# One hand-written order against another: 1498 operations of an attention and channel-mix kernel on five engines

## The chip, the cores and the metric

The kernel runs on one core of a Trainium2 chip. The metric is the device time of one execution in microseconds (us). A core has five engines that run at the same time, each through its own sequence of instructions: TensorE (PE, with its weight loads as PEld), VectorE (DVE), ScalarE (ACT), GpSimd (POOL) and SyncE (SP, which here only issues transfers). An instruction waits until what it reads is there and the buffer that it writes is free, and everything behind it on its engine waits with it. Transfers run on 16 DMA engines.

## The reference

For 8 batches of 8 heads, 576 positions and 64 features, linear attention with a feature map is followed by a channel mix with a shift by one position:

```python
def phi(x):
    proj = np.einsum('bhsd,df->bhsf', x, w_phi)
    proj = proj - np.max(np.abs(proj), axis=-1, keepdims=True)
    return np.concatenate([np.exp(proj), np.exp(-proj)], axis=-1)
q_p, k_p = (phi(q), phi(k))
kv = np.einsum('bhsf,bhsd->bhfd', k_p, v)
z = np.sum(k_p, axis=2)
num = np.einsum('bhsf,bhfd->bhsd', q_p, kv)
den = np.einsum('bhsf,bhf->bhs', q_p, z)[..., None] + 1e-06
...
xk = mu_k * x + (1.0 - mu_k) * x_prev
xr = mu_r * x + (1.0 - mu_r) * x_prev
k = np.maximum(xk @ w_k, 0.0)
v = k * k @ w_v
r = 1.0 / (1.0 + np.exp(-(xr @ w_r)))
return (r * v).astype(np.float32)
```

Here x is num / den with the heads side by side (512 wide); w_k is 512 x 1024, w_v 1024 x 512, w_r 512 x 512.

## The kernel before

The functions `add_load`, `add_edge`, `add_pair`, `add_moe` and `add_moe_edge` (from L312 on) make named operations. The text `ORDER` (L19) is one list of all 1498 names, written out in full by a search that is not part of the kernel. `Plan.order` (L143) reads it, and the last loop (L980) issues the operations in that sequence, so each engine's own sequence is what remains of the list when the other engines' names are left out. In a word such as `pb1/DVE`, what stands behind the slash is the engine, where there is a choice; `:1` is the PSUM buffer that the operation writes; `+2@3` puts two filler matmuls in front. A name that ends in `.d` stands for the landing of a transfer; except for `lk0.0.d` and `lq0.0.d`, which are casts, it issues nothing.

The work is 32 pairs of heads, four to a batch (pair n is of batch n // 4). For a pair:

- lk, lq, lv load k, q and v. lk and lq are always on POOL and write bfloat16 (L321); the loads of k, q for the very first pair (hk, hq) come on SP and ACT and are cast afterwards. lv is on POOL or SP (L327), in halves of a batch (three buffers), except that the first three loads of batch 0 are pair 0, pair 1 and pairs 2 and 3.
- The transposes of batches 0 and 1 are on TensorE (pt, L338) with copies out of PSUM (pa, pb, L346); those of the other six are DMA transposes by SP (tr, L352), two pairs each.
- kp and qp project k and q (L566); rk and rq reduce to the negative largest magnitude (L579, L584); ea and eb take exp of both signs of k (L605); em does it for the maxima of k (L591); mh, mt and mc bring the maxima of q across (L615, L620); qt projects q transposed and adds the maxima (L630, L636), qa and qb take exp (L643); va and vb scale v (L597); kv, kc, nd form the products (L656, L677); ra, rd divide (L685, L689). The last 64 of the 576 positions of a batch, for all its pairs, are handled by the edge operations tp, rt, mhe, mte, mce, eme, ekt, qte, eqe (L457 to L515).
- The result is transposed to put features on partitions: for pairs 0 to 7 by TensorE (xt, L715, copied by xe, xf), for the others by a DMA transpose on SP (xz, L700, with xu, L704 to L708). df takes the difference to the shifted position (L726), xa and xb mix (L732).

For a batch b, whose four pairs must all be mixed: h{b}.0 to .7 (L810) with rl (relu, L206, L208) and sq (square, L212, L214), r{b}.0 to .3 (L829) with th (tanh, L835), v{b}.0 to .3 (L843) with ob (L849) and the stores so on SP (L856). For each two batches the edge rows do the same once more: he, rle, sqe, re, the, ve, obe, soe (L897 to L942).

TensorE's 64-row operations are kp, qp, qt, kv, tp and qte; the others use all 128 rows. PSUM has three buffers P and two M, so h, r, v, pt, mt, xt and the like alternate between two.

Of the kernel before, what the change touches and what calls it, by code (L numbers as in the profile page):

```python
# [19 lines left out]
ones hk hq ident dve2 hk.d hq.d wphi wphi.d lk0.1 lk0.1.d lq0.1 lq0.1.d mus mus.d lk0.2 lk0.2.d dve3  # L20
lq0.2 lq0.2.d lv0.0/POOL lv0.0.d lk0.0.d/DVE lq0.0.d/ACT lv0.1/SP lv0.1.d pt0.0:0+9@0 lv0.2/SP
lv0.2.d pt0.1:1 pa0/DVE pb0/ACT tr0 dve1 tp0.0:0+1@2 kp0:1 rt0.0 qp0:2 rk0 eme0.0 mhe0.0/POOL ekt0.0
pt1.0:1+1@0 lk1.0 lk1.0.d pa1/ACT mte0.0:0 rq0 ea0 lq1.0 lq1.0.d pt1.1:1+2@2 pb1/DVE tr1 lk1.2
lk1.2.d eb0 kp1:2+2@2 tp0.1:0 lq1.2 lq1.2.d rt0.1 em0 rk1 qp1:1+1@1 ekt0.1 mh0/POOL eme0.1 wk.0
wk.0.d mt0:1+1@1 mc0/ACT mce0.0/DVE rq1 ea1 qt0:0+1@2 wk.1 wk.1.d wk.d pt2.0:1 qa0 pt2.1:0
mhe0.1/DVE mh1/POOL pa2/DVE pb2/DVE tr2 eb1 vb0/POOL pt3.0:1+2@3 pt3.1:0 pa3/DVE qb0 pb3/DVE tr3
va0/POOL mte0.1:1+1@3 qp2:2 mt1:0 rq2 qp3:1 mce0.1/ACT mc1/ACT em1 qte0.1:1 wr.0 wr.0.d qt1:0 eqe0.1
qte0.0:0 rq3 lv1.0/POOL lv1.0.d qa1 tp0.2:2 va1/POOL qb1 rt0.2 kp2:1+3@1 rk2 vb1/POOL ekt0.2
kv0:0+1@1 eqe0.0 pt4.0:1 kc0/DVE ea2 mhe0.2/POOL pt4.1:0 pa4/DVE kp3:0 pb4/DVE tr4 kv1:2 wr.1 wr.1.d
wr.d eb2 rk3 pt5.0:0 wv.0 wv.0.d pt5.1:1 eme0.2 qp4:1 pa5/DVE kc1/ACT mh2/POOL em2 rq4 nd0:2  # L30
mh3/POOL pb5/ACT tr5 wv.1 wv.1.d wv.d em3 mt2:0 pt6.0:1 ea3 mc2/DVE ra0 nd1:1 vb2/POOL pa6/DVE rd0
eb3 pt6.1:0 pt7.0:1 va2/POOL pb6/DVE tr6 qt2:2 pa7/ACT ra1 rd1 mte0.2:0 qa2 lk2.0 lk2.0.d pt7.1:1
mce0.2/DVE qp5:0 pb7/DVE tr7 qte0.2:0 lq2.0 lq2.0.d qb2 rq5 tp1.0:1 xt0:1 va3/POOL eqe0.2 kv2:2
rt1.0 xf0/ACT xe0/ACT kp4:0 mh4/POOL mt3:0 kc2/ACT rk4 xt1:1 df0/POOL mc3/ACT ekt1.0 nd2:2 ra2 ea4
vb3/POOL xe1/DVE qt3:1+1@0 rd2 mt4:0 xf1/ACT mc4/ACT df1/DVE qa3 xt2:1 xa0 kv3:2 eb4 mhe1.0/DVE
xe2/DVE mte1.0:0+1@0 xb0 kc3/ACT kp5:0 qb3 qt4:2 xa1 eme1.0 xf2/DVE nd3:1 rk5 mce1.0/ACT df2/POOL
qa4 ra3 qb4 rd3 lv1.2/POOL lv1.2.d ea5 xa2 xt3:0+7@1 qp6:2 xb1 qte1.0:1 xe3/ACT qp7:1 eb5 xf3/DVE
df3/DVE xa3 em4 qt5:0+1@0 eqe1.0 rq6 vb4/POOL h0.0:0 qa5 va4/POOL rq7 kp6:2 qb5 h0.1:1 rk6 mh6/POOL
kp7:1 rl0.1/ACT kv4:0 va5/POOL rl0.0/ACT tr2.0 tr2.0.d tr8 tr9 mt6:1 kc4/DVE ea6 h0.2:0 rk7 vb5/POOL
eb6 xb2 kv5:0+1@2 mc6/ACT sq0.0/ACT xb3 nd4:2 tr2.2 tr2.2.d tr10 tr11 em6 ea7 h0.3:1 kc5/DVE  # L40
vb6/POOL ra4 rd4 nd5:0 eb7 vb7/POOL rl0.3/DVE qt6:2 rl0.2/ACT ra5 qp8:1 rd5 qa6 lv2.0/SP lv2.0.d
sq0.1/POOL r0.0:1 rq8 qb6 va6/POOL qp9:0 h0.4:0 rq9 th0.0 sq0.3/POOL sq0.2/ACT qt7:2 kv6:1 rl0.4/DVE
qa7 lk3.0 lk3.0.d tp2.0:0 kc6/DVE h0.5:1 mh8/POOL rt2.0 qb7 va7/POOL xt4:0 rl0.5/ACT kp8:1 xf4/DVE
# [973 lines left out]
```

## Time and profile before

| what | value |
|---|---|
| device time, three runs | 277.23, 278.66 (median), 284.07 us |
| span of the profiled execution | 275.3 us |
| instructions | 8865 |
| first transpose on TensorE (pt0.0) | 5.2 us |
| second pair's transpose (pt1.0) | 7.6 us |
| first product of the channel mix (h0.0) | 39.6 us |
| last product ends, last engine instruction ends | 271.0, 271.5 us |
| granted TensorE clock | 1.000 |
| read from HBM, written | 33.62 MB, 9.44 MB |
| DMA transposes of q and k, on SP | 12, issue 2.4 to 5.9 us each |
| POOL load issues | 31, 0.56 to 0.81 us each |

The span is counted from the first to the last instruction of the profiled execution. The page gives no device time of that one execution beside it; the runs' times are from executions without the profiler. A busy share counts the time in which an engine executes; waiting and issuing from SP don't count. Matmuls overlap, so that a busy TensorE needn't be one at its peak.

### The profile page before, as it was taken

The numbers are of one execution on the slowest core, as the hardware profiler recorded it, in microseconds if no ns is written. First come the engines' busy times: TensorE is split into PE (matmuls) and PEld (weight loads), VectorE is DVE, ScalarE is ACT, GpSimd is POOL, SyncE is SP. The second block draws the span as 40 slices with busy tenths as digits, with TensorE's granted clock in tenths as the row PEclk, the third lists the DMA queues.
The fourth block names the chain that finished last, engine by engine and source line by source line (L and its number), as shares of the span: only waits on it lengthen the run. The fifth ranks groups of instructions, "written<-read, shape, count | busy, mean of one in ns | idle before, by whom it ended". The sixth has DMA issues, their size and how long they took to land.

```text
span 275.3 us, 8865 instructions
## 1 busy us (share of the span) xinstructions
PE 261.7 (95%) x3682; PEld 154.1 (56%) x3730; DVE 234.6 (85%) x388; ACT 223.1 (81%) x413; POOL 142.4 (52%) x193
## 2 busy tenths in 40 slices
PE   7899889999899999999999999999999999999993
PEld 3567656566555566555565666555566565444542
DVE  6999999999799989999999889998889897864222
ACT  3899999999899997899898999789987777616330
POOL 5799557976818682633459465821931611300200
PEclk9999999999999999999999999999999999999999
DMA  7999999599999899759699998981725324142134
GB/s 147 285 209 250 209 213 174 114 235 175 238 129 200 202 219 185 155 127 248 99 166 164 215 249 142 171 255 41 161 89 88 77 52 100 42 110 67 29 88 116
DMA packets 65817, 42.89 MB, mean 156 GB/s; under 512 B 47152, under 2 KB 57008, under 8 KB 65776
## 3 DMA queue, kind: packets, MB, share of 16 engines
q1 hardware_dynamic: 54496, 27.54, 49.3%
q0 software_dynamic: 11056, 14.42, 29.1%
q8 instruction: 29, 0.48, 0.8%
q10 hardware_dynamic: 224, 0.36, 0.5%
q14 instruction: 12, 0.10, 0.1%
HBM read 33.62 MB, written 9.44 MB: 156 GB/s over the span
## 4 chain that ended last, share of the span: by engine, by line
PE 75%; DVE 8%; ACT 6%; issue 4%; DMA 3%; POOL 2%; SPq 0%; POOLq 0%; ACTq 0%
PE ps_h L810 19%; PE ps_v L843 17%; PE ps_r L829 9%; PE ps_nd L677 5%; PE ps_kv L656 5%; DMA qkT<-nat 3%; PE ps_he L897 3%; PE ps_ve L929 3%; PE ps_k L566 2%; PE ps_qT L630 2%; PE ps_q L566 2%; PE ps_qT L636 2%; ACT k L605 2%; DVE nmk L579 2%; PE ps_f L292 1%
## 5 line engine op out<-in xcount | busy, mean ns | idle before, releaser
L597 POOL TENSOR_TENSOR v<-vt,v 128x576 bf16<-128x576 f32 x59 | 69.8, 1203 | 33.5 <-ACT v L591 31.1
L605 ACT ACTIVATE k<-ps_k 128x1024 bf16<-128x1024 f32 x64 | 64.8, 1047 | 1.3 <-DVE nmk L579 1.3
L643 ACT ACTIVATE q<-ps_qT 128x1024 bf16<-128x1024 f32 x64 | 63.8, 1054 | 1.8 <-PE ps_qT L636 1.7
L810 PE MATMUL ps_h<-xk,wk_bf 128*128 128x512 bf16 x235 | 60.5, 380 | 1.2
L843 PE MATMUL ps_v<-wv_bf,kk 128*128 128x512 bf16 x244 | 58.2, 379 | 0.6
L579 DVE TENSOR_REDUCE nmk<-ps_k 128x8 f32<-128x1024 f32 x32 | 38.8, 1217 | 1.8 <-PE ps_k L566 1.5
L584 DVE TENSOR_REDUCE nmq<-ps_q 128x8 f32<-128x1024 f32 x32 | 38.3, 1217 | 1.6 <-PE ps_q L566 1.4
L843 PEld LDWEIGHTS <-kk 128*128 128x128 bf16 x256 | 24.1, 98 | 27.3
L810 PEld LDWEIGHTS <-wk_bf 128*128 128x128 bf16 x256 | 22.7, 97 | 25.0 <-issue 0.7
L206 ACT ACTIVATE krelu<-ps_h 128x512 bf16<-128x512 f32 x48 | 28.8, 611 | 9.3 <-PE ps_h L810 9.3
L726 POOL TENSOR_TENSOR diff<-xs 128x576 bf16<-128x576 bf16 x15 | 20.2, 1346 | 28.8 <-ACT xs L706 12.7
L214 POOL TENSOR_TENSOR kk<-krelu 128x512 bf16<-128x512 bf16 x18 | 19.1, 1068 | 30.3 <-ACT krelu L206 26.6
L849 DVE SCALAR_TENSOR_TENSOR ob<-rt,ps_v 128x512 f32<-128x512 bf16 x32 | 21.7, 682 | 14.3 <-PE ps_v L843 12.7
L829 PE MATMUL ps_r<-wr_bf,xr 128*128 128x512 bf16 x116 | 31.1, 380 | 0.7
L835 ACT ACTIVATE rt<-ps_r 128x512 bf16<-128x512 f32 x32 | 19.7, 615 | 8.8 <-PE ps_r L829 8.7
L732 DVE SCALAR_TENSOR_TENSOR xk<-diff,mu_k_t,xs 128x576 bf16<-128x576 bf16 x32 | 26.7, 839 | 0.1
L689 DVE TENSOR_TENSOR x_sc<-ps_nd,rden 128x640 bf16<-128x640 f32 x32 | 26.0, 817 | 0.6
L732 DVE SCALAR_TENSOR_TENSOR xr<-diff,mu_r_t,xs 128x576 bf16<-128x576 bf16 x32 | 25.6, 806 | 0.1
L656 PE MATMUL ps_kv<-v,k 64*128 64x65 bf16 x1024 | 22.4, 190 | 0.5 <-ACT q L643 0.2
L566 PEld LDWEIGHTS <-qkT 64*128 64x128 bf16 x512 | 16.5, 94 | 11.0 <-issue 8.0
L656 PEld LDWEIGHTS <-k 64*128 64x128 bf16 x1024 | 19.3, 94 | 5.7 <-issue 1.8
L677 PE MATMUL ps_nd<-kv,q 128*128 128x65 bf16 x512 | 21.4, 193 | 0.0
(102 smaller groups left out, 414.3 us busy)
## 6 DMA issues: line engine op xcount, KB each, us to landing
out_dram<-ob SPq DMA_DIRECT2D x70, 128.0 KB, 2.5
vt<-in_v_dram SPq DMA_DIRECT2D x11, 576.0 KB, 6.1
nat<-in_k_dram POOLq DMA_DIRECT2D x6, 576.0 KB, 7.8
nat<-in_q_dram POOLq DMA_DIRECT2D x6, 576.0 KB, 8.0
vt<-in_v_dram POOLq DMA_DIRECT2D x4, 576.0 KB, 6.0
wk_bf<-in_moe_w_k_dram POOLq DMA_DIRECT2D x2, 512.0 KB, 11.4
wv_bf<-in_moe_w_v_dram POOLq DMA_DIRECT2D x2, 512.0 KB, 10.6
nat<-in_k_dram POOLq DMA_DIRECT2D x3, 288.0 KB, 6.9
```

The lines of the kernel that those rows point to most:

```text
L206: nc.scalar.activation(out_, in_, AF.Relu, scale=HALF)
L579: nc.vector.tensor_reduce(t[:, j, :], s["k"].rearrange("p a (g f) -> p (a g) f", f=128), axis=AX.X, op=ALU.max, apply_absolute_value=True, ...
L584: nc.vector.tensor_reduce(t[:, j, :], s["q"].rearrange("p a (g f) -> p (a g) f", f=128), axis=AX.X, op=ALU.max, apply_absolute_value=True, ...
L597: (nc.vector if eng == "DVE" else nc.gpsimd).tensor_tensor(vb[:, a, pn, :, 0:64], vt[b, a // 2][:, a % 2, :].rearrange("p (s d) -> p s d", ...
L605: nc.scalar.activation(s[f"k{pn}"], s["k"].rearrange("p a (g f) -> p (a g) f", f=128), AF.Exp, scale=(1.0 if pn == 0 else -1.0))
L643: nc.scalar.activation(t.rearrange("f x (a p) -> f x a p", a=2), s["qT"].rearrange("f a (x p) -> f x a p", p=64), AF.Exp, scale=(1.0 if pn ...
L656: nc.tensor.matmul(ps[:, hh, pn * 65:(pn + 1) * 65], lhsT=s[f"k{pn}"][r, c, :], rhs=vb[r, a, pn, 2 * g + par, :], start=(pn == 0 and c == ...
L677: nc.tensor.matmul(ps[:, bk, o * 65:(o + 1) * 65], lhsT=tail if sl < 2 else s[f"q{pn}"][:, 2 * G + h, :], rhs=s["kv"][:, h, pn, :], start= ...
L732: nc.vector.scalar_tensor_tensor(out=t[:, a, (b % 2) * S:(b % 2 + 1) * S], in0=s["d"], scalar=mu[:, a:a + 1], in1=xs[:, a, 0:S], op0=ALU.m ...
L810: nc.tensor.matmul(ps, lhsT=wk_bf[:, c, fc * 128:(fc + 1) * 128], rhs=xkt[bp][:, c, m0:m0 + 512], start=(c == 0), stop=(c == NDC - 1))
L829: nc.tensor.matmul(ps, lhsT=xrt[bp][:, c, m0 + ci * 128:m0 + (ci + 1) * 128], rhs=wr_bf[:, c, :], start=(c == 0), stop=(c == NDC - 1))
L843: nc.tensor.matmul(ps, lhsT=s["kk"][:, fc, ci * 128:(ci + 1) * 128], rhs=wv_bf[:, fc, :], start=(fc == 0), stop=(fc == NFC - 1))
```

## The change

Only the text `ORDER` differs. The set of names is the same, the 17 places with filler matmuls and their numbers too. What differs is the sequence on every engine and the engine of some operations:

| operation | before | after |
|---|---|---|
| lv | POOL 5, SP 12 | POOL 11, SP 6 |
| rl, rle | ACT 53, DVE 19 | ACT 49, DVE 23 |
| sq, sqe | ACT 28, DVE 26, POOL 18 | ACT 29, DVE 21, POOL 22 |
| va, vb | POOL 59, DVE 5 | POOL 55, DVE 9 |
| df | DVE 17, POOL 15 | DVE 15, POOL 17 |
| xu | ACT 12, POOL 10, DVE 2 | ACT 5, POOL 16, DVE 3 |
| xe, xf | ACT 6, DVE 10 | ACT 3, DVE 13 |
| kc | ACT 19, DVE 13 | ACT 21, DVE 11 |
| mc, mce | ACT 17, DVE 11 | ACT 12, DVE 16 |
| mh, mhe | POOL 22, DVE 6 | POOL 24, DVE 4 |
| pa, pb | ACT 4, DVE 12 | ACT 5, DVE 11 |
| cast of lq0.0 | ACT | DVE |

TensorE's sequence is close to the old one: most moves are by one to three places; tr7.2 now comes before tr7.0 on SP. The diff, cut to the parts that the text speaks of:

```diff
-ones hk hq ident dve2 hk.d hq.d wphi wphi.d lk0.1 lk0.1.d lq0.1 lq0.1.d mus mus.d lk0.2 lk0.2.d dve3
-lq0.2 lq0.2.d lv0.0/POOL lv0.0.d lk0.0.d/DVE lq0.0.d/ACT lv0.1/SP lv0.1.d pt0.0:0+9@0 lv0.2/SP
-lv0.2.d pt0.1:1 pa0/DVE pb0/ACT tr0 dve1 tp0.0:0+1@2 kp0:1 rt0.0 qp0:2 rk0 eme0.0 mhe0.0/POOL ekt0.0
-pt1.0:1+1@0 lk1.0 lk1.0.d pa1/ACT mte0.0:0 rq0 ea0 lq1.0 lq1.0.d pt1.1:1+2@2 pb1/DVE tr1 lk1.2
...
-qa7 lk3.0 lk3.0.d tp2.0:0 kc6/DVE h0.5:1 mh8/POOL rt2.0 qb7 va7/POOL xt4:0 rl0.5/ACT kp8:1 xf4/DVE
-xe4/DVE qp10:2 eme2.0 lq3.0 lq3.0.d r0.1:1 rk8 ekt2.0 mhe2.0/POOL r0.2:0 th0.1 rq10 sq0.4/POOL ea8
...
-rk11 ea10 lk4.0 lk4.0.d v0.1:0 qb8 mh10/DVE xa5 lv3.0/SP lv3.0.d eb10 xb5 kv9:0 xb4 em10 qt9:1
...
-ob5.3 xu29/ACT xu28/ACT rd30 nd31:0 the2 df28/POOL r6.0:0 xz30 xz30.d ra31 df29/DVE h6.1:1 th6.0
...
-xu31/ACT soe2 soe2.d df31/DVE r6.2:1 ob6.0 xb30 so6.0 so6.0.d r6.3:0 th6.2 xa31 v6.1:1 th6.3 xb31
-v6.2:0 ob6.1 so6.1 so6.1.d r7.0:1 ob6.2 xa30 so6.2 so6.2.d r7.1:0 th7.0 h7.0:1 th7.1 h7.1:0
...
+hk wphi mus wphi.d mus.d hq ident lv0.1/POOL lk0.1 lq0.1 lk0.1.d lq0.1.d lv0.1.d ones dve2 dve3 hk.d
+hq.d lk0.0.d/DVE lq0.0.d/DVE pt0.0:0+9@0 pa0/DVE dve1 pt0.1:1 pb0/ACT tr0 tp0.0:0+1@2 rt0.0 ekt0.0
+eme0.0 kp0:1 pt1.0:1+1@0 qp0:2 pa1/ACT rk0 ea0 eb0 rq0 lk0.2 lv0.0/POOL lq0.2 lk0.2.d lq0.2.d
+lv0.0.d em0 mhe0.0/POOL lk1.0 lq1.0 lk1.2 mh0/POOL lv0.2/POOL lk1.0.d pt1.1:1+2@2 pb1/DVE tr1
...
+wk.1 qa1 qb1 kv0:0+1@1 rk2 pa4/ACT ekt0.2 ea2 eme0.2 eb2 pt4.1:1 pt5.0:0 kc0/DVE pb4/DVE pa5/DVE tr4
+kp3:0 kv1:1 pt5.1:0 rk3 pt7.0:1 kc1/ACT qp4:2 pb5/DVE pa7/DVE pt6.0:0 mt2:1 nd0:1 em2 ea3 mc2/ACT
...
+xe4/DVE sq0.5/DVE r0.1:0 th0.1 kc7/DVE rk8 qp10:1 kp9:0 h0.6:1 rq10 rk9 lk3.0 mhe2.0/POOL lq3.0
+lk3.0.d df4/POOL mh8/POOL sq0.4/POOL lq3.0.d xa4 ea8 rl0.6/ACT eb8 r0.2:0 qp11:1 h0.7:1 em8 va8/POOL
...
+tr13 tr3.2.d tr14 tr15 xe5/DVE rk10 xf5/DVE sq0.7/POOL vb9/POOL va9/POOL mh10/POOL df5/POOL lk4.0
...
+qt30:2 th5.3 so4.3.d v5.3:0 rl6.0/ACT qa30 eb31 qb30 re2:1 the2 vb30/DVE kv30:1 kv31:2 qt31:0 ob5.3
+xz28 xz29 so5.2 so5.1 so5.0 xz29.d xz28.d r6.0:0 h6.1:1 xu28/ACT df28/POOL kc31/ACT th6.0 xu29/POOL
+df29/POOL kc30/DVE sqe2.1/DVE sq6.0/DVE rl6.1/DVE qa31 sq6.1/ACT qb31 h6.2:0 nd30:1 rl6.2/DVE xb29
+sq6.2/ACT h6.3:1 xb28 rl6.3/ACT sq6.3/ACT h6.4:0 rl6.4/DVE ra30 sq6.4/POOL nd31:2 h6.5:1 rl6.5/ACT
...
+r6.2:1 xu31/ACT th6.2 r6.3:0 v6.1:1 th6.3 v6.2:0 df31/DVE xb31 df30/DVE xa30 ob6.1 xb30 ob6.2 xa31
+so6.0 soe2 so6.0.d soe2.d r7.0:1 r7.1:0 th7.0 th7.1 h7.0:1 rl7.0/ACT sq7.0/DVE h7.1:0 h7.2:1
```

## The prediction

> **What bounds the kernel now.** I read the page's busy shares and slices first, then the sums by stretch of time, then the waits of TensorE, then the timeline of the first 14 us and of the end.
>
> Page, busy shares and three rows of slices:
>
> ```profile
> PE 261.7 (95%) x3682; PEld 154.1 (56%) x3730; DVE 234.6 (85%) x388; ACT 223.1 (81%) x413; POOL 142.4 (52%) x193
> PE   7899889999899999999999999999999999999993
> DVE  6999999999799989999999889998889897864222
> ACT  3899999999899997899898999789987777616330
> ```
>
> Three engines are near full for two thirds of the run. The sums by stretch (length, then busy time of each engine) tell them apart:
>
> ```profile
> 16.00:24.00 8.00, 7.38 (x177) 5.68 (x176) 7.98 (x13) 7.80 (x23) 7.68 (x15) 1.00 1.16 209
> 24.00:32.00 8.00, 7.19 (x168) 5.46 (x166) 7.88 (x15) 7.99 (x16) 7.21 (x9) 1.00 1.20 243
> 32.00:40.00 8.00, 6.86 (x111) 4.25 (x105) 7.86 (x16) 8.00 (x17) 2.63 (x3) 1.00 1.15 234
> 120.00:150.00 30.00, 29.63 (x429) 16.79 (x435) 28.91 (x45) 26.66 (x51) 16.91 (x21) 1.00 0.92 162
> 240.00:250.00 10.00, 9.95 (x46) 4.42 (x46) 6.04 (x9) 2.73 (x6) 0.67 (x1) 1.00 0.52 122
> ```
>
> From 16 to 40 us VectorE (third number) and ScalarE (fourth) have no room: 23.72 and 23.79 of 24 us. From 120 us TensorE is at 99% and the others are not. Busy is not peak, so I looked at the spacing of its weight loads: inside an MLP product (L810, L843, L829) they follow at 0.216 us throughout, and after 72 us no gap between two of them is longer than the spacing that the same neighbours always have. Before 72 us the gaps beyond that come to some 15 us. TensorE's waits on a named releaser after 40 us are one:
>
> ```profile
> PE ps_e L466 <- DMA qkT<-nat: 1.1, 1, 1.1
> PEld L466 <- DMA qkT<-nat: 1.2, 1, 1.2
> PEld L566 <- issue: 8.0, 20, 0.5
> ```
>
> The first two are the same stall (tp3.0, 71.6 us, on transpose tr3.2). The third isn't a wait for data: it is the step from 128-row to 64-row products, 0.52 us from load to load instead of 0.216.
>
> So: up to h0.0 (39.6 us) the end is set by VectorE and ScalarE together, behind the first transfers; after 72 us by TensorE's fixed work, 199 us of it. A saving after 72 us can't come from removing waits, because there are none; a delay before 40 us goes to the end in full.
>
> **What the Trainium skill says.** "SBUF — State Buffer", section "SBUF: two separate sides": the port pair that VectorE and GpSimd share is an exclusive lock for a whole instruction. The trace agrees but shows how little is left of it (minimum/median/maximum ns):
>
> ```profile
> L726 POOL TENSOR_TENSOR diff<-xs x15: 1269/1280/1736, 28.9 to 239.4; 128x576 bf16<-128x576 bf16 x15
> L597 POOL TENSOR_TENSOR v<-vt,v x59: 1158/1171/1694, 13.8 to 220.4; 128x576 bf16<-128x576 f32 x59
> ```
>
> "TensorEngine Tiling (Array Packing)", section "Key Properties": a change of tiling mode drains TensorE; the 0.52 us steps agree. "DMA: Bandwidth & Descriptors", section "Issuing engines are not separate DMA queues": loads from POOL and SP run on the same 16 engines, so another issuer saves issue time only; here a load takes POOL 0.56 to 0.81 us and SP 0.41 to 0.59.
>
> **The change part by part.** The same 1498 words; what counts is each engine's own sequence.
>
> 1. First loads. POOL now issues lv0.1 ahead of lk0.1 and lq0.1, lv0.0 ahead of lq0.2, and lv0.2 ahead of lq1.2; SP no longer loads v here. What is late next shows in the timeline:
>
> ```profile
> 2.15 0.56 POOL L321 DMA_DIRECT2D nat<-in_q_dram  x1
> 7.56 0.48 PEld L338 LDWEIGHTS <-nat 128*128 128x128 bf16 x5
> 8.26 0.69 ACT L200 COPY qkT<-ps_pt 128x640 bf16<-128x640 bf16 x1
> 8.68 1.22 DVE L584 TENSOR_REDUCE nmq<-ps_q 128x8 f32<-128x1024 f32 x1
> 8.84 1.95 ACT L605 ACTIVATE k<-ps_k 128x1024 bf16<-128x1024 f32 x2
> ```
>
> ```profile
> DMA to landing us min/median/max: 5.4/5.4/5.4
> ```
>
> The first line is lq0.1; 2.15 + 5.4 = 7.55, and pt1.0 starts at 7.56: it waits for nothing else. Behind pt1.0 stand pa1 (8.26) and ea0, eb0 on ScalarE, and, new, qp0, which the change puts behind pt1.0 on TensorE; rq0 on VectorE needs it. How late is lq0.1 now? At least the issue, 0.56; at most that and its place in the queue, 1.6: the loads lk0.1, lq0.1 and lk0.2 take 4.4, 5.4 and 6.4 us, 1.0 more for each place, so 2.15 + 0.56 + 6.4 = 9.1. With SP's two v loads gone the transfers may be quicker, down to 4.4: 7.1. That is -0.4 to +1.6; I take +1.2. ScalarE gets it whole (ea0 stands right behind pa1), VectorE less 0.28 (qp0 had that much to spare: 7.56 + 0.44 + 0.4 = 8.4 against 8.68). Through h0.0 I take **+1.1**. lq0.0's cast goes from ScalarE (0.67) beside lk0.0's to VectorE behind it (0.46 + 0.46): the second is done 0.1 to 0.15 later: **+0.15**. pt7.0 moves up before qp4 (about 22.7 with the delay) and needs lq1.2, now issued near 12.0 behind lv0.2: with today's 9.3 us to landing, 21.3, in time.
>
> 2. VectorE and ScalarE in the head. Adding up durations in each engine's sequence up to xa3, which h0.0 needs: VectorE -0.1, ScalarE up to qb3 -0.5, of which 0.67 is that cast, so +0.2 from ea0 on. **0**.
>
> 3. POOL in the head. 7.45, 7.68 and 7.21 of each 8 us from 8 to 32 are busy, and it gets two v issues (1.3), mhe0.1 (0.4) and wv.1 earlier, against wk.1 and wr.1 later: +1.6 up to mh1, +1.3 up to vb1. It stood idle for 2.95 us up to mhe0.0, and kv0 and kv1 had 2 and 0.3 us. Following its sequence, vb1 ends at 20.5 and mh2 at 23.4; with the 1.1 above their users come at 21.3 and 23.9. **0**, hidden by that very delay; without it 0.3.
>
> 4. The transposes. tr3.0 and tr3.2 wait for lq3.0, which comes at about the same place (behind mhe2.0 instead of mh8 and va7). lk4.0, issued at 64.3 into the middle of them, comes behind sq0.7 (1.04) and mh10 (0.4); lv3.0 goes to POOL, behind lk4.0 and va10. tr3.0 took 6.5 us, tr3.2 7.8, later ones as little as 4.6. tp3.0's stall of 1.3 can go to between 0 and 1.3: **-0.9**. Nothing else on TensorE waits for a transpose, so the other 11 save SP time only; it covers them with idle time (it waits 42.4 us for lk loads alone).
>
> 5. Ports. What POOL's instructions take above their medians, and VectorE's three slow xa and df, come to some 4 and 1.3 us, on VectorE all after 220 us, where it is idle 0.9 to 4 of each 10 us. **0**, at most -1.
>
> 6. TensorE's sequence. 61 groups of 64-row work instead of 62: **-0.3**. All else is the same work.
>
> 7. The second half. Up to each of obe0, rt5.0 and ob3.0 VectorE has 0.6 to 1.7 us less to do than before, ScalarE 1 to 5 less everywhere: no new wait there. From rt7.0 to ob6.2 VectorE has 3.6 us more (rl and df from others, va30 and vb30). kv30 needs vb30, now on VectorE behind rd28 and va30: about 0.4 late. nd30 and nd31 move from 225.7 and 229.8 in between h6.2 and h6.5, so rd31 ends 0.9 us later and xz31, xu31, df31, xb31 follow with no reserve. The end of that chain today:
>
> ```profile
> 245.60 0.69 DVE L849 SCALAR_TENSOR_TENSOR ob<-rt,ps_v 128x512 f32<-128x512 bf16 x1 [0.65 <-PE ps_v L843]
> 247.39 0.69 DVE L849 SCALAR_TENSOR_TENSOR ob<-rt,ps_v 128x512 f32<-128x512 bf16 x1 [1.10 <-PE ps_v L843]
> 248.00 0.81 DVE L732 SCALAR_TENSOR_TENSOR xk<-diff,mu_k_t,xs 128x576 bf16<-128x576 bf16 x1
> ```
>
> The last (xa30) ends at 248.8, when h7.0 starts: no reserve today either, and xa31 takes that place. New is xb30 behind ob6.1: 246.3 + 0.8 = 247.1 against r7.0 at 246.9, 0.3 late. Together **+0.7**; bounds 0 (VectorE's idle time takes it) and 3.6 (none does).
>
> 8. SP's sequence. so0.3 stands behind so1.0, xz9 behind xz10, xz18 and so2.2 behind xz19. Their users come 8 us or more later. **0**.
>
> Sum: 1.1 + 0.15 - 0.9 - 0.3 + 0.7 = +0.75; the profiled span of 275.3 becomes 276.1. The runs' median is 278.66 (277.23 to 284.07), 3.4 above that span; I carry the difference over: **279.4**.
>
> **Rivals.** (a) The aims pay: lq0.1 lands no later, the stall at 71.6 goes (1.3) with the step (0.3) and half a microsecond of the small gaps from 40 to 72: -2.1, 276.6. For: loads do stretch transposes. Against: only one transpose is waited for. Over 2% would need 5.6 us off a head whose two engines stay full. (b) Slower: VectorE sets the pace from rt7.0 on. Its waits for ps_v persist where they are, so the 3.6 us come on top, and the chain behind rd31 hands each of them to r7.0: with the head's 1.25 and 1.6 of further waits for nd30 and nd31, 281.7 span, 285.1. It decides once rd31 is about 5 us later than today's 237.8. For: no reserve at xb30 and xa31. Against: 11 us of idle VectorE from 180 to 250. (c) POOL falls 2 us behind at mh2, with mt2 holding nd0, pt6.1 and qt2: +2.75, 281.4.
>
> **How the numbers follow.** No change 0.60, (a) 0.14, (b) 0.20, (c) 0.06. Two per cent, 5.6 us, is about what a measurement of this kernel tells from none. Faster gets 0.05 of (a); slower 0.18 of (b) and 0.02 each of the first and of (c); the rest, 0.73, is the same. Range: low end 275.5, the sum of all low bounds (-2.0) and 2 us of the runs' spread; high end 285.5, which holds (b).
>
> **What would show it.** Right: pt1.0's first weight load near 8.7, h0.0 near 40.8, the tp3.0 stall under 0.5, no TensorE wait from 75 to 245, r7.0 within 1 us of h0.0's shift. Wrong: h0.0 before 39.6; or named waits of TensorE on VectorE after 186.

## The result, and the profile after

The changed kernel is slower. Compared on one chip its median is 288.1 us (285.95 to 288.78, four runs) against 280.1 us (277.23 to 284.07, four runs) for the kernel before, and the ratio of the times is 1.032, 95% interval 1.024 to 1.040. That is above the forecast of 279.4 us and above its range. Some executions of either kernel are slow, several us longer at a lower granted clock: the ratios leave them out, so that 1.032 isn't 288.1 / 280.1, and e6 below was profiled in one (span 295.0 us), so that only single instructions and short stretches of it are read.

The profiled execution has a span of 287.0 us where before has 275.3, so 11.7 us more. These two executions are not alike. The one of the changed kernel took 288.8 us, the longest of its four. In every execution with both figures the time is about 1.8 us above the span, so the one of before took some 277.1 us (an estimate from that difference), about its shortest. By the ratio a typical difference is 9 us (3.2% of 280); the rest of the 11.7 is spread between executions.

The page of the changed kernel, the lines that answer to those of before, with the row of the granted clock:

```profile
PE 267.4 (93%) x3730; PEld 154.2 (54%) x3730; DVE 241.1 (84%) x393; ACT 221.8 (77%) x390; POOL 149.7 (52%) x217
...
PE   7899778999949999799999999999999999999994
...
DVE  6889999999947998999899999989889797965422
...
PEclk9999999999998999999999999999999999999999
```

The twelfth slice (79 to 86 us) has a 4 for TensorE and for VectorE, where before has a 9; one slice later the clock has an 8. TensorE's busy time is 5.7 us above that of before, but this can't be read as longer work: the page of before lacks the records of 48 matmuls (x3682, with 3730 weight loads). The sums by stretch (length, then busy time of PE, PEld, DVE, ACT and POOL, granted clock, DMA share, GB/s) look closer:

```profile
16.00:24.00 8.00, 7.27 (x165) 5.41 (x165) 7.56 (x13) 8.00 (x22) 7.49 (x13) 1.00 1.16 240
...
80.00:84.00 4.00, 0.56 (x17) 0.41 (x13) 0.37 (x1) 1.42 (x5) 0.00 (x0) 1.00 1.15 174
84.00:88.00 4.00, 3.49 (x52) 1.92 (x53) 4.00 (x7) 2.17 (x3) 0.00 (x0) 0.67 0.38 74
120.00:150.00 30.00, 30.00 (x429) 16.90 (x427) 28.39 (x40) 25.92 (x47) 18.54 (x31) 1.00 0.87 163
```

One of these stretches in the kernel before:

```profile
80.00:84.00 4.00, 3.95 (x80) 2.41 (x81) 4.00 (x6) 3.77 (x11) 2.06 (x2) 1.00 1.20 154
```

From 80 to 84 us the engines of the changed kernel stand almost still, only ScalarE works for 1.42 us; the DMA engines are at work. Behind it TensorE's clock is 0.67. From 120 us on TensorE is as full as before, so next to nothing is lost there. TensorE's waits on a named releaser name two new ones (us in total, times, longest):

```profile
PE ps_qT L630 <- DVE x_sc L689: 3.9, 1, 3.9
PE ps_m L620 <- DVE mhl L616: 1.9, 1, 1.9
```

These are qt11 at 84.5 us and mt16 at 116.9 us. After 186 us there is one named wait left, 0.5 us. How late each operation starts against before, in these two profiles: h0.0 1.6 us, v0.0 3.2, kv10 2.4, kp13 8.3, h2.0 10.4, ve3.1 (the last product) 11.8. So the time goes in four places: the head (+3.2), the stretch from kv10 to kp13 (+5.9), mt16 (+2.2), and 1.4 us over the whole second half; at tp3.0 0.8 us come back.

**The first place, 80 us.** VectorE's timeline before and after, then SP's (start and length in us; in brackets the idle time before it and what ended it), then the landing times of the transposes of x on SP from 68 to 95 us:

```profile
75.80 0.82 DVE L689 TENSOR_TENSOR x_sc<-ps_nd,rden 128x640 bf16<-128x640 f32 x1
```

```profile
83.63 0.82 DVE L689 TENSOR_TENSOR x_sc<-ps_nd,rden 128x640 bf16<-128x640 f32 x1 [4.02 <-DMA xs<-x_sc]
```

```profile
73.49 1.49 SPq L700 DMA_TRANSPOSE xs<-x_sc  x1
```

```profile
DMA to landing us min/median/max: 2.6/2.6/10.0
```

The first two lines are rd9. In the changed kernel it waits for a landing of an xs transpose, and the only one under way is xz8, issued at 73.49 and landed 10.0 us later, while the loads lk4.0, lv3.0 and lq4.0 (576 KB each) were under way too. But rd9 doesn't read what xz8 writes. It writes an x buffer, of which there are three. If they went round in turn, rd9 would get that of rd6, read long ago. In the built program they don't: which buffer an operation gets is fixed when the program is built, and here x9 has the address of x8, which xz8 is reading. In the program of before, with so0.2 ahead of xz8, it has that of x6. Everything on VectorE behind rd9 waits too, and qt11, which needs the PSUM buffer that rd9 frees.

**The second, 114 us.** mh16 on GpSimd before, then on VectorE after, then GpSimd after:

```profile
103.22 0.19 POOL L615 CAST mhl<-nmq 128x16 bf16<-128x16 f32 x1
103.49 0.22 POOL L616 TENSOR_TENSOR mhl<-nmq,mhl 128x16 bf16<-128x16 f32 x1
```

```profile
114.40 1.25 DVE L615 CAST mhl<-nmq 128x16 bf16<-128x16 f32 x1
115.68 1.21 DVE L616 TENSOR_TENSOR mhl<-nmq,mhl 128x16 bf16<-128x16 f32 x1
```

```profile
114.15 1.50 POOL L327 DMA_DIRECT2D vt<-in_v_dram  x2
115.66 1.19 POOL L597 TENSOR_TENSOR v<-vt,v 128x576 bf16<-128x576 f32 x1
```

Where VectorE has an mh in the kernel before, its two instructions take 0.165 and 0.174 us. Here the first ends with GpSimd's two load issues (115.65), the second with va15 (116.85). The change moved both sides: mh16 from GpSimd to VectorE, lv4.0 and lv4.2 from SP to GpSimd.

**The head.** xa3, the last operand of h0.0, takes 1.61 us instead of 0.82, beside va4 on GpSimd (40.97 to 42.15). Before, then after:

```profile
38.87 0.82 DVE L732 SCALAR_TENSOR_TENSOR xk<-diff,mu_k_t,xs 128x576 bf16<-128x576 bf16 x1
```

```profile
41.16 1.61 DVE L732 SCALAR_TENSOR_TENSOR xk<-diff,mu_k_t,xs 128x576 bf16<-128x576 bf16 x1
```

### The profile page after: what moved, and what is told of

It reads as the page before. It is cut to its first block, busy times and chain, and to the rows that moved or that the text cites. A ratio compares the mean times of both kernels' runs of the same rounds, so it can differ in the third digit from the quotient of the medians.

```text
span 287.0 us, 8892 instructions
## 1 busy us (share of the span) xinstructions
PE 267.4 (93%) x3730; PEld 154.2 (54%) x3730; DVE 241.1 (84%) x393; ACT 221.8 (77%) x390; POOL 149.7 (52%) x217
## 4 chain that ended last, share of the span: by engine, by line
PE 65%; ACT 12%; DVE 8%; DMA 7%; POOL 3%; issue 2%; SPq 2%; POOLq 0%; DVEq 0%; ACTq 0%
PE ps_h L810 17%; PE ps_v L843 16%; PE ps_r L829 8%; PE ps_nd L677 5%; ACT q L643 4%; PE ps_kv L656 4%; ACT k L605 4%; DMA xs<-x_sc 4%; DMA nat<-in_q_dram 3%; PE ps_he L897 3%; PE ps_qT L630 2%; PE ps_ve L929 2%; PE ps_q L566 2%; PE ps_qT L636 2%; DVE nmq L584 2%
## 5 line engine op out<-in xcount | busy, mean ns | idle before, releaser
L597 POOL TENSOR_TENSOR v<-vt,v 128x576 bf16<-128x576 f32 x55 | 64.1, 1183 | 22.3 <-ACT v L591 22.2
L810 PE MATMUL ps_h<-xk,wk_bf 128*128 128x512 bf16 x256 | 64.0, 386 | 0.8 <-DVE xk L732 0.8
L843 PE MATMUL ps_v<-wv_bf,kk 128*128 128x512 bf16 x256 | 59.1, 379 | 0.0
L214 POOL TENSOR_TENSOR kk<-krelu 128x512 bf16<-128x512 bf16 x20 | 21.0, 1052 | 54.5 <-ACT krelu L206 34.0
L726 POOL TENSOR_TENSOR diff<-xs 128x576 bf16<-128x576 bf16 x17 | 22.5, 1322 | 28.7 <-DVE xr L732 12.1
L206 ACT ACTIVATE krelu<-ps_h 128x512 bf16<-128x512 f32 x43 | 25.8, 601 | 8.4 <-PE ps_h L810 7.5
L829 PE MATMUL ps_r<-wr_bf,xr 128*128 128x512 bf16 x128 | 32.2, 380 | 0.0
L849 DVE SCALAR_TENSOR_TENSOR ob<-rt,ps_v 128x512 f32<-128x512 bf16 x32 | 21.8, 682 | 11.9 <-PE ps_v L843 10.6
L835 ACT ACTIVATE rt<-ps_r 128x512 bf16<-128x512 f32 x32 | 19.3, 604 | 14.0 <-PE ps_r L829 13.7
L566 PEld LDWEIGHTS <-qkT 64*128 64x128 bf16 x512 | 16.5, 94 | 11.9 <-issue 10.4
```

Source lines behind the costliest of these rows:

```text
L597: (nc.vector if eng == "DVE" else nc.gpsimd).tensor_tensor(vb[:, a, pn, :, 0:64], vt[b, a // 2][:, a % 2, :].rearrange("p (s d) -> p s d", ...
L810: nc.tensor.matmul(ps, lhsT=wk_bf[:, c, fc * 128:(fc + 1) * 128], rhs=xkt[bp][:, c, m0:m0 + 512], start=(c == 0), stop=(c == NDC - 1))
L829: nc.tensor.matmul(ps, lhsT=xrt[bp][:, c, m0 + ci * 128:m0 + (ci + 1) * 128], rhs=wr_bf[:, c, :], start=(c == 0), stop=(c == NDC - 1))
L843: nc.tensor.matmul(ps, lhsT=s["kk"][:, fc, ci * 128:(ci + 1) * 128], rhs=wv_bf[:, fc, :], start=(fc == 0), stop=(fc == NFC - 1))
```

## The experiments

The theory after the first comparison: four separate causes, each in one place, of which the buffer that rd9 waits for is the largest. The rivals, that something else delays each place, stand in the expectations. For all kernels but e6 and the two small ones, one table from the profiles, in us: when v0.0 starts (what the head and the stretch behind it cost), how long it is from kv10 to kp13, from v1.2 to mt16, and from h2.0 to ve3.1. It keeps the places apart, with one exception: how long rd9 waits depends on when xz8 lands, so a stretch that begins late looks short (e2, e4). In the kernel before mt16 comes ahead of v1.2. The ratio is that of the times to those of the kernel before on the same chip. The intervals of e2, e3, e4 and e7 overlap with that of the changed kernel: their times alone show no gain, and what they show is in the stretches. e1, e5 and e8 stand clear of it.

| kernel | v0.0 | kv10 to kp13 | v1.2 to mt16 | h2.0 to ve3.1 | span | ratio (95% interval) |
|---|---|---|---|---|---|---|
| before | 63.0 | 9.1 | | 156.5 | 275.3 | 1 |
| after | 66.2 | 15.0 | 3.8 | 157.8 | 287.0 | 1.032 (1.024 to 1.040) |
| e1 store first | 69.2 | 9.7 | 3.8 | 156.9 | 283.4 | 1.017 (1.013 to 1.020) |
| e2 fillers | 66.5 | 13.2 | 3.8 | 156.9 | 286.3 | 1.021 (1.011 to 1.032) |
| e3 mh16 | 66.1 | 14.4 | 1.5 | 158.2 | 284.7 | 1.017 (1.006 to 1.027) |
| e4 first loads | 66.9 | 13.4 | 3.8 | 156.8 | 286.6 | 1.020 (1.013 to 1.028) |
| e5 two | 67.6 | 9.5 | 1.5 | 157.2 | 281.9 | 1.007 (1.004 to 1.010) |
| e7 head | 64.5 | 13.7 | 3.8 | 156.8 | 282.8 | 1.020 (1.008 to 1.032) |
| e8 head and two | 64.2 | 9.5 | 1.5 | 157.4 | 277.2 | 0.998 (0.994 to 1.002) |
| e10 before, xz8 | 63.2 | 13.2 | | 156.5 | 280.8 | medians 282.1 and 279.5 us |
| e11 middle | 63.0 | 10.6 | | 156.5 | 277.5 | 0.999 (0.996 to 1.003) |

### e1: the store ahead of xz8

```diff
-qb10 th0.3 eb12 xz8 v0.3:1
+qb10 th0.3 eb12 so0.2 so0.2.d xz8 v0.3:1
...
-xz11 so0.2 kp14:1
+xz11 kp14:1
...
-h1.7:0 so0.2.d mc14/DVE
+h1.7:0 mc14/DVE
```

> One edit to the changed kernel: on SP the store so0.2 goes ahead of the transpose xz8, as it does in the kernel before. Theory A (buffer of x): in the changed kernel rd9 was given the x buffer of rd8, which is free only when transfer xz8 has landed (10.0 us after its issue); with this edit rd9 gets the buffer of rd6, which xt6 has long read. Then rd9 doesn't wait (4.0 us now), qt11 starts right behind mte3.0, and h1.0 and h1.1 run at 0.216 us from load to load instead of 0.427: 3.7 + 9 x 0.21 = 5.6 us less, about 282.5 us. Rival B (the transfers are late in any case, since tr4.0 holds SP for its load until 86 us): the wait moves on to what xz8, xz9 and xz10 deliver, and less than 2 us come back: 286 us or more.

Measured: x9 has the address of x6 again, rd9 doesn't wait, and the stretch from kv10 to kp13 goes from 15.0 to 9.7 us, 5.3 us less. TensorE's lines for h1.0 and h1.1, changed kernel first, then this one:

```profile
85.79 3.34 PE L810 MATMUL ps_h<-xk,wk_bf 128*128 128x512 bf16 x8
```

```profile
84.52 1.90 PE L810 MATMUL ps_h<-xk,wk_bf 128*128 128x512 bf16 x8
```

Theory A holds; xz8, xz9 and xz10 are issued later here and it costs nothing, so rival B falls. The span fell by 3.6 us only, since this execution lost 3.0 us more before v0.0 (lq0.1 landed later, and the clock fell to 0.63 from 46 to 50 us).

### e2: fillers in the idle time

```diff
-mte3.0:0 qt11:2
+mte3.0:0 qt11:2+14@0
```

> One edit to the changed kernel: 14 filler products of 512 columns on TensorE between mte3.0 and qt11, where it now idles 3.9 us. The wait of rd9 stays. Theory A2 (TensorE's clock is lowered after it has idled): with the fillers the clock stays, h1.0 and h1.1 go at 0.216 us from load to load instead of 0.427, and 1.9 us come back: about 286.2 us, with qt11 where it was, near 84.5 us. Rival (the 0.427 us are waits of the products for data of VectorE): they stay, 288.1 us, or slower by what the fillers run over.

Measured: rd9 starts at 83.65 us, as in the changed kernel (83.63), but the clock stays at 1.00 and h1.0 and h1.1 take 1.90 us:

```profile
83.25 3.18 PE L292 MATMUL ps_f<-ones 128*128 128x512 bf16 x14 [0.71 <-ACT mTe L200]
...
87.46 1.90 PE L810 MATMUL ps_h<-xk,wk_bf 128*128 128x512 bf16 x8
```

So the 0.427 us were the clock (0.50 on record there, 1.00 here) and not waits for data; the products alone, which start 1.7 us later here, would not tell the two apart. The fillers gain no time: they end 1.9 us after qt11 could have started, and kp13 begins at 89.3 us, 89.1 in the changed kernel. The 13.2 instead of 15.0 us from kv10 to kp13 only say that kv10 came 2.0 us later, because xa5 was held (see e5), while rd9 starts at the same time. What the clock cost is read from the changed kernel itself (in each line, the third number from the end is the granted clock):

```profile
84.00:86.00 2.00, 1.49 (x47) 1.20 (x48) 2.00 (x5) 0.78 (x1) 0.00 (x0) 0.83 0.31 60
86.00:88.00 2.00, 2.00 (x6) 0.71 (x5) 2.00 (x3) 1.39 (x3) 0.00 (x0) 0.50 0.45 88
88.00:90.00 2.00, 2.00 (x30) 1.02 (x29) 0.54 (x2) 1.30 (x4) 1.14 (x2) 0.81 1.11 207
```

Over 2 us each, 0.17, 0.50 and 0.19 of the clock are missing, together 1.7 us; of the 5.3 that leaves 3.6 for the wait itself. The Trainium skill, "TensorE: Matmul & The Clock Gate", section "What's actually happening", says that after an idle window of some 3.4 us the array runs at half its clock until it has been busy for such a window. The trace agrees on the half (after 3.9 us idle, 0.427 us from load to load instead of 0.216) and on how long it stays: 1.7 us lost at half clock are 3.4 us. On the idle time before it, it doesn't: in e4 and e7 qt11 waits 2.5 and 2.8 us only, and the granted clock falls to 0.50 all the same (at 86 to 88 and at 82 to 84 us), so the measurement decides.

### e3: mh16 on GpSimd

```diff
-rd13 mh16/DVE df11/POOL
+rd13 df11/POOL
...
-ob1.0 rq17 rk16
+ob1.0 rq17 mh16/POOL rk16
```

> One edit to the changed kernel: mh16 (two instructions on 128x16) on GpSimd, behind xu11, as in the kernel before, instead of VectorE. Theory C (shared port): the two took 1.25 and 1.21 us on VectorE instead of 0.17 each since GpSimd held the port with two load issues and a va; on GpSimd they end near 111.2 us, mt16 doesn't wait (2.2 us now beyond the usual spacing): about 286.0 us. Rival (VectorE or another operand is late there anyway): nd14 or kv15 waits in its place, less than 0.7 us comes back: 287.4 us or more.

Measured: the wait of mt16 is gone, 2.2 us from v1.2 to mt16, and 2.3 us at the end of the profile. Nothing else waits in its place.

### e4: the first loads as before

```diff
-hq ident lv0.1/POOL lk0.1 lq0.1 lk0.1.d lq0.1.d lv0.1.d ones dve2 dve3 hk.d hq.d
+hq ident lk0.1 lq0.1 lk0.1.d lq0.1.d ones dve2 dve3 hk.d hq.d lv0.1/SP lv0.1.d lv0.2/SP lv0.2.d
...
-lk0.2 lv0.0/POOL lq0.2
+lk0.2 lq0.2 lv0.0/POOL
...
-lk1.2 mh0/POOL lv0.2/POOL lk1.0.d
+lk1.2 mh0/POOL lk1.0.d
```

> One part of the changed kernel undone: lv0.1 and lv0.2 are issued by SP again, so that lk0.1 and lq0.1 are the first loads of GpSimd, and lq0.2 goes ahead of lv0.0. Theory D (the first loads set the head): pt1.0's last weight load near 7.9 us instead of 8.6, rk2 1.3 earlier, h0.0 near 40.0 instead of 41.2: about 286.8 us. Rival E (the head is late by VectorE's own sequence): h0.0 moves by less than 0.4 us, 287.7 us or more.

Measured: the last weight load of pt1.0 at 7.87 instead of 8.60 us, rq2, h0.0 and xa3 each 0.67 us earlier. The first loads are worth 0.7 us at h0.0: half of theory D, more than rival E. The rest of the head's loss is elsewhere. At the end nothing is seen of it in this profile (TensorE's clock was 0.57 from 44 to 48 us, and xa5 was held, see e5).

### e5: the store and mh16 together

The two diffs of e1 and e3 in one kernel.

> Two edits to the changed kernel together: so0.2 ahead of xz8 on SP, and mh16 on GpSimd behind xu11. If the two losses are separate and lie on the path, they add up: 5.7 + 2.2 = 7.9 us off the span of 287.0, 279.1 us, still 3.8 us (1.4%) above the kernel before, whose rest is the head. If the second only takes up slack that the first makes (or the other way round), the sum falls short by more than 1 us.

Measured: both gains are there in full, 5.5 us from kv10 to kp13 and 2.2 us to mt16. They are separate. The span is 281.9 and not 279.1, because the same order lost 2.2 us more in another place, on xa5 (VectorE, then GpSimd):

```profile
72.98 3.05 DVE L732 SCALAR_TENSOR_TENSOR xk<-diff,mu_k_t,xs 128x576 bf16<-128x576 bf16 x1
```

```profile
71.81 1.17 POOL L597 TENSOR_TENSOR v<-vt,v 128x576 bf16<-128x576 f32 x1 [0.63 <-ACT v L591]
72.93 0.76 POOL L327 DMA_DIRECT2D vt<-in_v_dram  x1
73.72 1.18 POOL L597 TENSOR_TENSOR v<-vt,v 128x576 bf16<-128x576 f32 x1
74.83 0.79 POOL L321 DMA_DIRECT2D nat<-in_q_dram  x1
```

xa5 starts as va10 ends and is held over lv3.0 (moved to GpSimd by the change), vb10 and most of lq4.0. In the changed kernel's profile it is not held (VectorE, then va10):

```profile
71.62 0.81 DVE L732 SCALAR_TENSOR_TENSOR xk<-diff,mu_k_t,xs 128x576 bf16<-128x576 bf16 x1
```

```profile
70.45 1.18 POOL L597 TENSOR_TENSOR v<-vt,v 128x576 bf16<-128x576 f32 x1 [0.61 <-ACT v L591]
```

Ten profiles have this order here. To the nanosecond, xa5 starts 0 to 8 ns before va10 ends in five of them (after, e1, e3, e7, e8) and takes 0.81 us; it starts 0 to 25 ns behind that end in the other five (e2, e4, e5, e6, e11) and takes 3.03 to 3.05 us.

### e6: va15 ahead of the loads

```diff
-lv4.0/POOL so0.3 xz12 so0.3.d lv4.2/POOL
+va15/POOL lv4.0/POOL so0.3 xz12 so0.3.d lv4.2/POOL
...
-the0 va15/POOL qt16:1
+the0 qt16:1
```

> One edit to the changed kernel: on GpSimd va15 goes ahead of the loads lv4.0 and lv4.2 instead of behind them, so that the first instruction of mh16 on VectorE meets va15 and the second one the two load issues. Theory C1 (a load issue of GpSimd holds the shared port just as its arithmetic does): both instructions are stretched again, mh16 ends near 116.8 us, the wait of mt16 stays, no gain. Theory C2 (only the arithmetic holds it): the first takes about 1.0 us, the second 0.18, mh16 ends near 115.5 us and 1.3 us come back.

Measured: the copy takes 0.97 us and ends with va15, the subtraction behind it 0.175 us, though a load issue is running beside it. From v1.2 to mt16 it is 2.5 instead of 3.8 us. That is C2's reading, but C2 can't say why the copy waited for two issues in the changed kernel, in five profiles with the same numbers.

This profile also shows how far the wait of tp3.0 can go. Its transpose tr3.2, issued at 69.88 us just ahead of lk4.0, landed after 18.3 us (6.7 in the changed kernel's profile):

```profile
88.22 0.39 PE L466 MATMUL ps_e<-wph,qkT 64*128 64x128 bf16 x4 [13.50 <-DMA qkT<-nat]
```

The edit comes 50 us later in the order, so it isn't the cause; what is stays open.

### e7 and e8: the head of before

Everything up to h0.0 in the order of the kernel before, the rest as changed; the words are those of the two orders, only the seam is new. e8 has the diffs of e1 and e3 as well.

> The changed kernel with the order of the kernel before, engines and buffers too, for everything up to h0.0 (the first 40 us), and the changed order from there on. Theory G (the head lost 3 us by the order of VectorE's and TensorE's work, of which the first loads are only a part): xa3 ends near 39.7 us instead of 42.8, and 3 us come back to the end: span 284.0. Rival H (what is gained early is lost again at the wait for xz8, whose landing is set by the load queues): less than 1 us at the end, span 286 or more.

> The order of before up to h0.0, then the changed order with so0.2 ahead of xz8 and mh16 on GpSimd. If the three causes add up (3.1 + 5.7 + 2.2 = 11.0 us), the span is near 276.0, within 1 us of the kernel before (275.3): the rest of the changed order, transposes, second half and all, is worth nothing either way. If a fourth loss was hidden behind these, it shows here, at 278 or more.

Measured, e7: xa3 ends at 40.5 instead of 42.8 us and is not held (0.82 us). Of these 2.3 us 1.7 arrive at v0.0, because kp6 now waits 1.4 us for rq6 at the seam of the two orders. So G holds at v0.0, with less than its 3 us; H falls. The span is 4.2 us shorter, more than G's 3, because the wait of qt11 is 2.8 instead of 3.9 us in this profile and the second half 1.0 us shorter; that part is not the head's. Measured, e8: 277.2 instead of 276.0, a ratio of 0.998. Three edits bring the changed order to the time of before. No fourth loss of any size is hidden; what is left to before, 1.9 us of span, is that seam (1.2 at v0.0) and the second half (0.9), against an execution of before that was about its shortest; in the times nothing is left.

### e9 and e12: the port by itself

Two small kernels with the instructions in question, in loops; the first with issues alone and multiplications alone, the second with both in turn. From the second (M is a multiplication, I a load issue, n the number of small memsets ahead on VectorE):

```python
for i, n in enumerate((16, 18, 20, 22, 24, 26)):
    part(i, "MIMIM", n, mixes)
for i, n in enumerate((20, 24, 28, 32)):
    part(6 + i, "MIIM", n, pairs)
```

> The disputed cost by itself; everything of the reference is left out, the output is zeros. VectorE runs the two instructions of mh (a copy from float32 to bfloat16 and a subtraction of two SBUF operands, 128x16, 16 of each) and the mixing instruction (128x576, 4): first alone, then each beside four load issues of GpSimd, then each beside three multiplications of 128x576 of GpSimd. Theory C3 (the port that the two engines share is taken by GpSimd's arithmetic and by its load issues alike): every form shows instructions of 1 us and more in both companies. C4 (a load issue holds it only for part of its time, and against some forms): beside issues only some instructions, or only the copy, go beyond 0.25 us, while beside the multiplications the subtraction and the mixing wait for whole instructions of 1.2 us. C5 (the port has no part in it): the durations are those alone, 0.17, 0.18 and 0.8 us, everywhere.

> Again the disputed cost by itself; the reference's work is left out, the output is zeros. GpSimd runs multiplication, load issue, multiplication, load issue, multiplication without a gap; VectorE starts four mixing instructions (128x576) behind 16 to 26 small memsets, so that the first meets the end of the first multiplication or the load issue behind it. Then multiplication, two load issues, multiplication, with three times the pair of mh behind 20 to 32 memsets. Theory P (a load issue between two multiplications doesn't give the port free, where VectorE's instruction was asked for before the multiplication had ended): some of the first mixing instructions take about 3 us, as xa5 did, and the first copy of mh behind two issues about 1.25 us, as in the changed kernel. Theory Q (each GpSimd instruction holds the port for itself alone): nothing takes longer than one multiplication and itself, 2.0 us for the mixing instruction, and an instruction that starts beside an issue is stretched by 0.1 us at most; the 3.05 us of xa5 and the 1.25 us of mh16 beside the issues then stay open.

Measured, e9: alone 0.175 (copy), 0.174 (subtraction) and 0.82 us (mixing). Beside load issues four copies of 16 take 0.27 to 0.29, the other two forms nothing more. Beside multiplications all three wait: 1.1 to 1.2 us for the small ones, 1.7 for the mixing, which gets in at the end of each multiplication. C4, then: an issue alone holds almost nothing.

Measured, e12: P is right that VectorE doesn't get in at an issue between two multiplications, but not about which instruction meets this. In all six parts the first mixing instruction, which starts before the first multiplication ends, gets in behind it and takes 1.40 to 1.60 us. The second starts 0.65 us behind that end, beside the last 0.04 to 0.17 us of the issue, and takes 3.95 to 4.08 us. VectorE, then GpSimd, in the first part:

```profile
2.69 1.60 DVE L44 SCALAR_TENSOR_TENSOR xo<-xa,mu,xb 128x576 bf16<-128x576 bf16 x1
4.33 4.08 DVE L44 SCALAR_TENSOR_TENSOR xo<-xa,mu,xb 128x576 bf16<-128x576 bf16 x1
```

```profile
2.41 1.27 POOL L58 TENSOR_TENSOR po<-pf,pg 128x576 bf16<-128x576 f32 x1
3.63 0.87 POOL L61 DMA_DIRECT2D vt<-in_v_dram  x1
4.52 1.28 POOL L58 TENSOR_TENSOR po<-pf,pg 128x576 bf16<-128x576 f32 x1
5.74 0.74 POOL L61 DMA_DIRECT2D vt<-in_v_dram  x1
6.50 1.28 POOL L58 TENSOR_TENSOR po<-pf,pg 128x576 bf16<-128x576 f32 x1
```

It ends at 8.41, 0.62 us behind the last multiplication: two whole multiplications and the issue between them pass it by, though for 0.70 us of that issue no multiplication runs. The copy of mh that starts beside the first of two issues takes 1.15 us and ends with the second, and the subtraction behind it 1.29 us, to the end of the multiplication: the 1.25 and 1.21 us of mh16. A subtraction that starts beside the first issue takes 0.18. So the two long instructions of mh16 are shown apart from everything else, and that a mixing instruction can be held across an issue as xa5 is. Open are the rule and the length: xa5 is let in behind one multiplication (3.05 us), the mixing instruction of e12 only behind two; in e6 the one behind mh16, which starts 0.16 us behind va15 beside an issue, with a second issue behind it and no multiplication, takes 0.81 us; and no run says why the subtraction slips in where the copy doesn't.

### e10: the cause put into the kernel before

```diff
-so0.2 so0.2.d xt6:0 ... xe6/DVE ekt3.0 xz8 xz8.d xe7/DVE
+xz8 xz8.d so0.2 so0.2.d xt6:0 ... xe6/DVE ekt3.0 xe7/DVE
```

> One edit to the kernel before, the reverse of the first experiment: on SP xz8 goes ahead of so0.2. With it rd9 gets the x buffer of rd8, as in the changed kernel. Theory A: rd9 waits until xz8 has landed. It is issued near 70 us behind tr3.2 and lv3.0; with 3 to 10 us to landing it is there between 73 and 80, where rd9 is due near 77: between nothing and 4 us of wait, and about as much at the end, more by 1.9 if TensorE idles over 3 us. No wait of rd9 on a landing at all would refute it. Rival B: the order of SP alone costs nothing, 0 us and no such wait.

Measured: rd9 waits for xz8, which was issued at 70.18:

```profile
79.82 0.82 DVE L689 TENSOR_TENSOR x_sc<-ps_nd,rden 128x640 bf16<-128x640 f32 x1 [2.65 <-DMA xs<-x_sc]
```

The granted clock falls too (0.58 and 0.57 from 82 to 86 us, again 1.7 us lost), and the stretch from kv10 to kp13 takes 13.2 instead of 9.1 us. The span is 5.5 us longer, 1.3 of it at tp3.0 and kv10. Counted as the ratios are, the time is 281.5 and 282.6 us in two runs, against 277.1 to 281.3 us in ten of the kernel before: 2.6 us between the medians (282.1 and 279.5). Two runs give this price only roughly. The mechanism is shown: one swap on SP, of two operations that exchange no data, makes rd9 wait in the kernel before too.

### e11: only the part that should pay

The order of before, with the changed one from kv8 to nd10 only (and the store first).

> The kernel before, with the changed order only from kv8 to nd10 (62 to 79 us), where lk4.0 comes behind sq0.7 and mh10, and with so0.2 ahead of xz8 as before. Theory: this is the part of the change that pays. The stall of tp3.0 falls from 1.3 us to 0.9 or less, nd10 comes 1.0 to 1.6 us earlier, and nothing later takes it back: span 274.0 instead of 275.3, a ratio of 0.995. Rival: the gain is taken back by the next wait: 1.000. xa5 on VectorE may lose 2.2 us to GpSimd's port there in some executions, as it did in three of the runs.

Measured: a ratio of 0.999, no gain. In the profile tp3.0 still waits for its transpose (2.0 us), the granted clock falls behind that wait (0.77, 0.50 and 0.87 from 72 to 78 us), and xa5 is held (3.03 us). Neither this nor e8 beats the kernel before, and no other kernel here does.

## Why the forecast was wrong, step by step

The sum was +0.75 us. Measured are +11.7 between the two profiles and some 9 by the ratio. By the forecast's own steps, with the sizes of the profiles:

1. *First loads, +1.1 and +0.15.* pt1.0's first weight load was forecast near 8.7 us. It comes at 7.81; only the last of the five waits for lq0.1, until 8.60, nearly the forecast time:

```profile
7.81 0.23 PEld L338 LDWEIGHTS <-nat 128*128 128x128 bf16 x4 [0.26 <-DMA nat<-in_k_dram]
8.60 0.10 PEld L338 LDWEIGHTS <-nat 128*128 128x128 bf16 x1 [0.56 <-DMA nat<-in_q_dram]
```

What it is worth at h0.0 is 0.7 (e4), not 1.1. A fair size, on the high side.

2. and 3. *VectorE, ScalarE and GpSimd in the head, 0.* Wrong. xa3 ends 3.1 us late; 0.7 are the loads, 0.8 xa3's wait for va4. Of the other 1.6 the order of the head has 0.8 to 1.6: e7 with the head of before takes back 2.3 us in all, and the five profiles with that head have xa3 ending at 39.7 to 40.5 us by themselves. Which operation is to blame was not taken apart. VectorE is busy for 22.3 of the 24 us from 16 to 40, before for 23.7, and is later all the same: adding up durations in sequence leaves out the idle time that a new sequence makes.
4. *Transposes, -0.9.* In the profile after, tp3.0's stall fell from 1.3 to 0.5, as forecast. That is luck: with this order it lay between nothing and 2.0 us in nine profiles and was 13.5 us in the tenth (e6), and e11 shows no gain.
5. *Ports, 0, at most -1.* The second step that failed. I bounded it by the stretches that the trace of before has, so by what was to be gained. What the change could lose was left out: a two-operand or copying instruction that lands beside a run of GpSimd's. Measured: 2.2 us at mt16 (e3), 0.8 at xa3, and 2.2 at xa5 in five of ten profiles. The Trainium skill, "SBUF — State Buffer", section "SBUF: two separate sides", on which the forecast drew, speaks of a lock for one whole instruction; e12 shows 3.95 to 4.08 us for one of 0.82, and there the measurement decides.
6. *61 groups instead of 62, -0.3.* Too small to be seen among the rest.
7. *The second half, +0.7.* About right: h2.0 to ve3.1 is 0.3 to 1.7 us longer in the eight profiles of the table with the changed order there. Rival (b) is false: TensorE waits on nothing of VectorE after 186 us.
8. *SP's sequence, "so0.3 stands behind so1.0, xz9 behind xz10, xz18 and so2.2 behind xz19. Their users come 8 us or more later. 0."* The step that failed most: 5.3 us (e1), and e10 makes it from the kernel before. It missed a pair, xz8 ahead of so0.2, and asked only who uses what a moved operation delivers. It didn't ask whose buffer the move would give to whom, and put that at nothing without counting through the three x buffers. The wait (3.6) brings its own follow-up, 3.4 us at half clock (1.7).

The rivals: (a) did not come about, nor did (c), since mh2 ends at 23.1 us, forecast 23.4, and TensorE waits for no mh of GpSimd; and the slower end that I did see, (b), was not the one. The condition "no TensorE wait from 75 to 245" was the one that told: it is broken at 84 and at 117 us.

The last term, 3.4 us from span to device time, was no constant either: one and the same execution has 1.8 us (288.8 for a span of 287.0). The 3.4 compared one execution's span with the median of others.

## What to carry to other kernels

When operations are only reordered, look at what the new order gives out, not only at who uses what: in the built program, compare for each buffer which earlier user it now waits for. Price a move onto an engine by what its neighbours hold there: in runs of GpSimd arithmetic with load issues between, a VectorE copy or two-operand instruction can wait for more than one of them. And where TensorE stands idle for some 2 us or more, reckon with a lower clock behind it: here it came after all five waits of 2.5 us and more and after two of nine from 1.8 to 2.3 us, and cost 1.7 us except in e6, where it stayed for longer.

## What the runs showed of the hardware that I had not expected

- A load issue of GpSimd costs VectorE nearly nothing by itself (copy +0.1 us), but between two multiplications it did not let VectorE in: 3.95 to 4.08 us for a mixing instruction of 0.82, six times of six.
- Whether xa5 is held turns on a few nanoseconds: 0.81 us where it starts 0 to 8 ns before va10 ends, 3.03 to 3.05 us where it starts 0 to 25 ns behind, five times each, from the same order.
- The granted clock also fell where no wait of TensorE lasted over 0.9 us: in three of seven profiles with the changed head (e1, e4, e5), to 0.50 to 0.55 over 2 us between 46 and 50 us. TensorE was busy for 5.6 to 5.7 of the 8 us from 38 to 46 in all three, but also in the changed kernel itself, whose clock stayed at 1.00, so what decides isn't in this share.
- The nine falls of the clock outside e6 each lost 1.7 us, after waits from 0.8 to 3.9 us (in e1, e3, e5, e7, e10, e11, twice in e4, and in the changed kernel).
- A 128x640 transpose on SP landed after 2.6 us at 89 us, and after 10.0 us at 73 us, with three loads of 576 KB under way.
